# A routed row of 1088 bytes in place of 1032, with the filling written by the operation that writes the row's index

## The chip, the core and the metric

The kernel runs on one core of a Trainium2 chip. The metric is the device time of one execution, in microseconds (us). Engines are named as in the profile: PE (matrix), PEld (its weight loads), DVE (vector), ACT (scalar activation), POOL (GpSimd, which also writes the descriptors of scattering transfers) and SP (which issues most other transfers). Each engine works through its own instructions strictly in their order.

## The reference

```python
def reference(x, filt_r, filt_i, expert_emb, tau, w1, w2):
    # x: (8, 2496, 256); a spectral filter along the sequence
    X = np.fft.rfft(x, axis=1)
    y = np.fft.irfft(X * (filt_r + 1j * filt_i)[None], n=2496, axis=1)
    x = y.reshape(19968, 256)
    # routing to one of 8 experts, each 256 -> 1024 -> 256
    xn, en = x / norm(x), expert_emb / norm(expert_emb)
    logits = xn @ en.T / tau
    expert_idx = argmax(logits, 1)
    gate_w = softmax(logits)[range(N), expert_idx]
    for e in range(8):
        mask = expert_idx == e
        h = maximum(x[mask] @ w1[e], 0)
        out[mask] = gate_w[mask, None] * (h @ w2[e])
    return out
```

## The kernel before

The eight batches are eight groups g = 0 to 7. For each, the spectral filter runs in three stages: `conv_s1` (input transform), `conv_s2` (second transform, the filter and its way back) and `conv_sb` (last transform, then routing). The buffers SD and ZD in DRAM carry data between the stages. `conv_sb` takes a batch in 11 tiles of two blocks of 117 tokens. For a tile, PE makes y; ACT squares the two blocks with a sum (L587, twice, with the operation's result thrown into the part of the row where the low half comes later); DVE makes a power-of-two scale rr from the sums (L590, L592); ACT writes the scaled upper fp16 half into `rows[:, i, 0:D]` (L559, for i = 0 and then i = 1, called first and second scale below); DVE writes the lower half (L562, also twice). POOL's iota (L596) writes the token's index behind the two halves; a reciprocal on DVE (L699) later writes the gate beside it. PE transposes the row (L606) and multiplies it by the experts' embeddings (L621). For every chunk of four tiles, `route` finds the expert and the place, and eight scattering transfers (L711, one for each block, six for the last chunk of three tiles) write the rows into the table XS in DRAM, sorted by expert. They stand as a train on POOL.

The experts' work is done in slots of 256 rows: SP loads a slot's rows from XS with a transposing transfer (xT, L834), PE does the two products (L865 into ph, L892 into po), ACT and DVE make h between them (L871, L872), and POOL scatters the result to the output (L900). While the slots of group g run, the filter of group g+1 runs between them; behind group 7 come slots of 128 rows from what is left over.

At the start no slot can run yet: group 0's filter, `conv_s1` of group 1 and the preparation of the weights (`weight_halves`: maxima on DVE, L242 and L243, an all-reduce over the partitions on POOL, L246, scales and halves on DVE, ACT and POOL, L267 to L272) run alone. This part, some 210 us long, is called the head here. In it the order of ACT and PE is that in which the code is written; everywhere else, and on DVE, POOL and SP throughout, a scheduler orders the instructions. It also derives waits from which bytes of a tile an instruction touches.

A row buffer is `rowp.tile([P, 2, ROW], F16)`: two rows of ROW fp16 numbers behind each other in each partition. Of an XS row, 1024 bytes are the two halves, then 4 bytes of index and 4 bytes of gate.

Of the kernel before, what the change touches and what calls it, by code (L numbers as in the profile page):

```python
# [15 lines left out]
I32 = mybir.dt.int32  # L16
# [9 lines left out]
S = NA * NB39  # L26
NK2 = 20
A3 = 3
TOK = A3 * NB39
NAG = (NA + A3 - 1) // A3  # L30
D = 256
E = 8
F = 1024
ROW = 516

GROUPS = (1,) * 8
QUOTA = 256
# [19 lines left out]
def moe_spectral_kernel(  # L57
# [16 lines left out]
    nc = tc.nc  # L74
# [233 lines left out]
    ZD = [dram.tile([P * NK2, n * D], F32, name=f"ZD{g}") for g, n in enumerate(GROUPS)]  # L308
    XS = dram.tile([XROWS, ROW // 2], I32, name="XS")
    XS16 = XS.bitcast(F16)  # L310
# [13 lines left out]
    def widths(g):  # L324

        return NAG * GROUPS[g] // 2, NK2 * GROUPS[g] // 2
# [20 lines left out]
    def buf_at(g, buf):  # L347
        def at(t, k, half):
            if GROUPS[g] == 2:
                return buf[t * 120:t * 120 + k].rearrange("p (j c) -> p j c", j=2)  # L350
            if half:
                return buf[t * 120:t * 120 + k].unsqueeze(1)
            return buf[t * 240:(t + 1) * 240].rearrange("(j p) c -> p j c", j=2)
        return at
# [4 lines left out]
    def load(q, g, pool, tag, t, ap, rows, full):  # L359
        it = pool.tile([P, 2, D], F32, tag=tag, name=f"{tag}{g}_{t}")  # L360
        got = []
        for h, k, m in whole(g, ap, t, rows, full):
            q.dma_start(it[:k, h], m)  # L363
            got.append((h, it[:k, h].rearrange("p j c -> p (j c)")))
        return got
# [3 lines left out]
    def split(hi, lo, pieces):  # L369

        got = []
        for h, a in pieces:
            k, w = a.shape
            o = h.start * D
            xh, xl = hi[:k, o:o + w], lo[:k, o:o + w]
            nc.scalar.copy(xh, a)
            nc.vector.tensor_tensor(out=xl, in0=a, in1=xh.bitcast(F32), op=ALU.subtract)
            got.append((h, (xh, xl)))
        return got

    def pair(nm):
        return [cw.tile([P, 2 * D], F32R, tag="hl", bufs=XYB, name=f"{nm}_{i}") for i in range(2)]

    def asides(nm):

        return [rowp.tile([P, 2, ROW], F16, tag="rows", name=f"{nm}_{i}").rearrange("p j c -> p (j c)")
                .bitcast(F32R)[:, :2 * D] for i in range(2)]

    def parts_of(c, tag):

        k = c.shape[0]
        tmp = cw.tile([P, P], F32R, tag="hl", bufs=XYB, name=f"{tag}t")[:k]
        lo = const.tile([k, P], F32R, tag=f"{tag}l", name=f"{tag}l")
        nc.scalar.copy(tmp, c)
        nc.vector.tensor_tensor(out=lo, in0=c, in1=tmp.bitcast(F32), op=ALU.subtract)
        hi = const.tile([k, P], F32R, tag=tag, name=f"{tag}h")
        nc.scalar.copy(hi, tmp.bitcast(F32))
        return hi, lo
# [120 lines left out]
    def conv_sb(g):  # L519

        nb = GROUPS[g]
        NTL, _ = widths(g)

        def load_v(t):
            return load(nc.sync, g, cf, "f", t, buf_at(g, ZD[g]), freqs, 120)

        yield W_GAP
        vin = {t: load_v(t) for t in range(3)}
        yield W_GAP
        parts, out_rows = [], []  # L530
        chunks = {}
        yp = {}
        yts = {}

        def part():

            if parts and next(parts[0], None) is None:
                parts.pop(0)
            if out_rows:
                out_rows.pop(0)()  # L540

        if g == G_SB:
            cons["csb"] = parts_of(cons["csb"], "csb")
        for s in range(NTL + LPL):
            if s + 3 < NTL:
                vin[s + 3] = load_v(s + 3)
            if g >= G_SB:
                for u in (0, 1) if s == 0 else (s + 1,):
                    if u < NTL:
                        vin[u] = split(*pair(f"vp{g}_{u}"), vin[u])  # L550
            part()

            t = s - 1
            if 0 <= t < NTL:
                ck = chunks[t // CHUNK]
                rows, rr, y = ck["rows"][t % CHUNK], ck["rr"], yp.pop(t)
                for i in range(2):
                    u = t % CHUNK * 2 + i
                    nc.scalar.activation(rows[:, i, 0:D], y[:, i], AF.Copy, scale=rr[:, u:u + 1])  # L559
                for i in range(2):  # L560
                    u = t % CHUNK * 2 + i
                    nc.vector.scalar_tensor_tensor(out=rows[:, i, D:2 * D], in0=y[:, i], scalar=rr[:, u:u + 1],  # L562
                                                   in1=rows[:, i, 0:D], op0=ALU.mult, op1=ALU.subtract)
            t = s
            if t < NTL:
                c = t // CHUNK
                if t % CHUNK == 0:
                    n = 2 * min(CHUNK, NTL - t)
                    chunks[c] = {
                        "t0": t,  # L570
                        "n": n,
                        "rows": [],
                        "ssq": rt.tile([P, NTC], F32, tag="ssq", name=f"ssq{g}_{t}"),
                        "rr": rt.tile([P, NTC], F32, tag="rr", name=f"rr{g}_{t}"),
                    }
                ck = chunks[c]
                rows = rowp.tile([P, 2, ROW], F16, tag="rows", name=f"rows{g}_{t}")
                ck["rows"].append(rows)
                ssq, rr = ck["ssq"], ck["rr"]
                u = t % CHUNK * 2  # L580
                y = ps_y.tile([P, 2, D], F32, tag="y", name=f"y{g}_{t}")
                for h, vt in vin.pop(t):
                    product(y[:, h].rearrange("p j c -> p (j c)"), cons["csb"], vt)
                yp[t] = y
                for i in range(2):

                    nc.scalar.activation(rows[:, i, D:2 * D], y[:, i], AF.Square, accum_out=ssq[:, u + i:u + i + 1])  # L587

                q = rt.tile([P, 2], I32, tag="q", name=f"q{g}_{t}")
                nc.vector.tensor_scalar(out=q, in0=ssq[:, u:u + 2].bitcast(I32), scalar1=24, scalar2=None,  # L590
                                        op0=ALU.logical_shift_right)
                nc.vector.tensor_scalar(out=rr[:, u:u + 2].bitcast(I32), in0=q, scalar1=-(2.0 ** 23),  # L592
                                        scalar2=194.0 * 2.0 ** 23, op0=ALU.mult, op1=ALU.add)

                (b, ag), _ = tiles(g, t)
                nc.gpsimd.iota(rows.bitcast(I32)[:, :, D:D + 1].rearrange("p j o -> p (j o)"),  # L596
                               pattern=[[S if nb == 2 else TOK, 2]], base=b * S + ag * TOK, channel_multiplier=1)
            yield W_SB
            part()
            t = s - 2  # L600
            if 0 <= t < NTL:
                rows = chunks[t // CHUNK]["rows"][t % CHUNK]
                tp = ps_c.tile([P, 2, 4, P], F16, tag="c", name=f"tp{g}_{t}")
                for i in range(2):
                    for j in range(4):
                        nc.tensor.transpose(tp[:, i, j], rows[:, i, j * P:(j + 1) * P], ident)  # L606
                yT = cy.tile([P, 2, 4, P], F16, tag="yT", name=f"yT{g}_{t}")
                nc.vector.tensor_copy(yT, tp)
                yts[t] = yT

            t = s - LPL
            if t >= 0:
                ck = chunks[t // CHUNK]
                n = ck["n"]
                if t % CHUNK == 0:
                    ck["lp"] = ps_r.tile([P, NTC, 2 * E], F32, tag="r", name=f"lp{g}_{t}")
                for i in range(2):
                    u = t % CHUNK * 2 + i
                    yT = yts[t][:, i]
                    for j in range(4):  # L620
                        nc.tensor.matmul(ck["lp"][:, u], yT[:, j], ent[:, j] if j < 2 else enz[:, j - 2],  # L621
                                         start=(u == 0 and j == 0), stop=(u == n - 1 and j == 3))
                if t % CHUNK * 2 + 2 == n:
                    parts.append(route(g, out_rows, **ck))
            yield W_SB
        while parts or out_rows:
            part()
            yield W_SB
        if g == NG - 1:
            yield from zero_rows(state["base"])  # L630
# [160 lines left out]
    def zero_rows(cnt):  # L791

        zr = cst.tile([P, ROW], F16, tag="st", name="zr")
        nc.vector.memset(zr, 0.0)
# [310 lines left out]
```

## Time and profile before

| what | value |
|---|---|
| median of 3 runs | 1499.54 us (1493.44 to 1501.6) |
| the profiled execution, its own time | 1499.08 us |
| its span, first to last instruction | 1497.2 us |
| PE busy | 1301.8 us, 87% of the span |
| mean granted PE clock | 0.924 of full speed |
| instructions | 31982 |

The profile is one execution. A share of busy time is a mean over the head, the stages with slots and filter side by side, and the end with slots alone.

### The profile page before, as it was taken

To read this page: it belongs to the slowest core of one execution; us is meant where nothing else is said; L and a number is where in the kernel's file an instruction comes from. 1 tells how busy PE (TensorE), PEld (TensorE's weight loads), DVE (VectorE), ACT (ScalarE), POOL (GpSimd) and SP (SyncE) were. 2 spreads that over 40 slices of the span, in tenths; PEclk is the share of its full clock that TensorE was granted. 3 is DMA by queue.
4 is the path that set the end of the run, shared out by engine and by line. 5 is a ranking of instruction groups with operands and counts; after the bars stand their busy time and mean duration, and the time that the engine had idled before them with its cause. 6 is when DMAs were issued, how large, how long until landed. Compare 5 with 4: busy or idle time off the path is not lost.

```text
span 1497.2 us, 31982 instructions
## 1 busy us (share of the span) xinstructions
PE 1301.8 (87%) x10956; PEld 988.2 (66%) x10956; DVE 873.5 (58%) x2841; ACT 693.7 (46%) x1578; POOL 548.7 (37%) x614
## 2 busy tenths in 40 slices
PE   5644557998997998899979988997999789999997
PEld 1212235766765776686658666865787578899997
DVE  2558765563474757575648555664658432266664
ACT  2435554543562665375437634662665122333332
POOL 0021454245524543552445254525433431222222
PEclk7876678999998999999989999999999889999999
DMA  8865375646774775577457746674753222122211
GB/s 273 302 213 200 118 211 158 187 133 189 215 188 130 205 217 156 166 220 183 140 166 201 195 121 185 195 192 124 200 169 92 76 67 54 50 49 48 49 45 40
DMA packets 230494, 229.16 MB, mean 153 GB/s; under 512 B 126089, under 2 KB 172497, under 8 KB 228405
## 3 DMA queue, kind: packets, MB, share of 16 engines
q1 hardware_dynamic: 200908, 151.93, 37.7%
q0 software_dynamic: 26400, 60.07, 12.8%
q10 hardware_dynamic: 3017, 15.02, 3.0%
q8 instruction: 92, 1.51, 0.4%
q14 instruction: 77, 0.63, 0.1%
HBM read 121.61 MB, written 84.84 MB: 138 GB/s over the span
## 4 chain that ended last, share of the span: by engine, by line
PE 61%; issue 15%; POOL 3%; DMA 2%; ACT 1%; DVE 1%; another core or an unknown queue 1%; POOLq 0%; SPq 0%; ACTq 0%; DVEq 0%
PE po L892 22%; PE ph L865 21%; PE y L403 5%; PE s L403 5%; POOL out_dram L900 3%; PE tp L606 2%; PE sa L408 2%; PE s L408 2%; DMA f<-ZD 1%; PE lp L621 1%; PE sa L512 1%; DMA ZD<-z 1%; DVE xs L460 0%; DMA f<-in_filt 0%
## 5 line engine op out<-in xcount | busy, mean ns | idle before, releaser
L892 PE MATMUL po<-W,h 128*128 128x256 f16 (+1 forms) x3864 | 519.8, 279 | 27.9 <-issue 27.5
L892 PEld LDWEIGHTS <-h 128*128 128x128 f16 x3864 | 375.5, 100 | 132.4 <-issue 85.3
L865 PE MATMUL ph<-xT,W 128*128 128x256 f16 x3072 | 414.8, 279 | 30.9 <-issue 18.7
L872 DVE SCALAR_TENSOR_TENSOR h<-ph,h 128x512 f16<-128x512 f32 (+1 forms) x388 | 232.0, 598 | 277.6 <-ACT h L871 240.6
L865 PEld LDWEIGHTS <-W 128*128 128x128 f16 x3072 | 300.1, 100 | 129.0 <-issue 91.4
L871 ACT ACTIVATE h<-ph 128x512 f16<-128x512 f32 (+1 forms) x388 | 203.4, 525 | 378.8 <-PE ph L865 205.4
L900 POOL DMA_INDIRECT out_dram<-o,meta x161 | 171.5, 1065 | 359.0 <-ACT o L899 319.4
L711 POOL DMA_INDIRECT XS<-rows,ixi x176 | 176.6, 1004 | 172.4 <-issue 136.2
L403 PE MATMUL y<-f,csb_sb 120*128 120x512 f32 (+1 forms) x192 | 101.2, 612 | 39.8 <-DVE rows L562 17.7
L494 POOL TENSOR_TENSOR yy<-yy,xs 128x512 f32<-128x512 f32 x70 | 94.3, 1349 | 109.1 <-DVE xs L460 69.5
L363 POOL DMA_DIRECT2D in<-in_x x84 | 66.9, 797 | 154.9 <-PE s L403 113.4
L403 PE MATMUL s<-in,c_sb 117*128 117x512 f32 (+1 forms) x192 | 111.1, 672 | 12.8 <-DMA in<-in_x 8.1
L865 PE MATMUL ph<-xT,wp 128*128 128x128 f16 x1584 | 104.9, 219 | 0.2
L865 PEld LDWEIGHTS <-wp 128*128 128x128 f16 x1584 | 96.7, 98 | 3.2 <-issue 0.7
L587 ACT ACTIVATE rows<-y 128x256 f16<-128x256 f32 x176 | 66.0, 384 | 64.7 <-PE y L403 58.8
L559 ACT ACTIVATE rows<-y,rr 128x256 f16<-128x256 f32 x176 | 73.9, 473 | 46.8 <-DVE rr L592 44.7
L426 ACT COPY s<-s 128x512 f32<-128x512 f32 x88 | 51.5, 586 | 91.4 <-PE s L403 43.5
L458 DVE TENSOR_TENSOR yy<-s,f 128x256 f32<-128x256 f32 x160 | 60.9, 419 | 52.5 <-ACT xs L487 39.4
L562 DVE SCALAR_TENSOR_TENSOR rows<-y,rr,rows 128x256 f16<-128x256 f32 x176 | 77.1, 478 | 22.5 <-ACT rows L559 19.8
L853 DVE COPY wp<-W 128x1024 f16 x132 | 62.1, 471 | 45.3 <-PE ph L865 44.8
L899 ACT ACTIVATE o<-po,meta 128x256 f32<-128x256 f32 x161 | 69.4, 475 | 34.2 <-PE po L892 26.7
L460 DVE SCALAR_TENSOR_TENSOR xs<-xs,sgn_sb,f 128x256 f32<-128x256 f32 x160 | 82.0, 551 | 0.0
(170 smaller groups left out, 1397.0 us busy)
## 6 DMA issues: line engine op xcount, KB each, us to landing
f<-in_filt SPq DMA_DIRECT2D x160, 256.0 KB
a<-SD SPq DMA_DIRECT2D x80, 256.0 KB
ZD<-z SPq DMA_DIRECT2D x80, 256.0 KB
SD<-s SPq DMA_DIRECT2D x80, 240.0 KB
f<-ZD SPq DMA_DIRECT2D x80, 240.0 KB
in<-in_x POOLq DMA_DIRECT2D x70, 234.0 KB
W<-in_w ACTq DMA_DIRECT2D x14, 1024.0 KB
XS<-rows,ixi POOLq DMA_INDIRECT x176
```

Of the source, the lines that this page charges most:

```text
L403: nc.tensor.matmul(out_, c[:a.shape[0]], a, start=True, stop=True)
L460: nc.vector.scalar_tensor_tensor(out=o, in0=i, scalar=sgn_sb[:, k2:k2 + 1], in1=f, op0=ALU.mult, op1=ALU.mult)
L494: nc.gpsimd.tensor_tensor(out=yy, in0=yy, in1=xs, op=ALU.add)
L559: nc.scalar.activation(rows[:, i, 0:D], y[:, i], AF.Copy, scale=rr[:, u:u + 1])
L562: nc.vector.scalar_tensor_tensor(out=rows[:, i, D:2 * D], in0=y[:, i], scalar=rr[:, u:u + 1], in1=rows[:, i, 0:D], op0=ALU.mult, op1=ALU.s ...
L711: i = nc.gpsimd.indirect_dma_start(out=XS, out_offset=bass.IndirectOffsetOnAxis(ap=ix, axis=0), in_=src, in_offset=None)
L865: last["pe"] = nc.tensor.matmul(ph[:, fi, :size], wp[:, k * 2 + wh, fi * P:(fi + 1) * P], xT[:, xh * 2 + k], start=(c == 0), stop=(c == 5))
L871: nc.scalar.activation(h[:, 0, :, :size], ph[:, :, :size], AF.Relu)
L872: hd = nc.vector.scalar_tensor_tensor(out=h[:, 1, :, :size], in0=ph[:, :, :size], scalar=0.0, in1=h[:, 0, :, :size], op0=ALU.max, op1=ALU. ...
L892: nc.tensor.matmul(self.po[:, s], self.hs[fp][:, hh, fi, s * P:(s + 1) * P], self.Wp[:, off + wh * 1024:off + wh * 1024 + D], start=(fp == ...
L899: nc.scalar.activation(o, self.po[:, s], AF.Copy, scale=self.meta[:, s, 1:2])
L900: i = nc.gpsimd.indirect_dma_start(out=out, out_offset=bass.IndirectOffsetOnAxis(ap=self.meta[:, s, 0:1].bitcast(I32), axis=0), in_=o, in_ ...
```

## The change

A row in XS and in the row buffers has 544 fp16 numbers, 1088 bytes, instead of 516 (1032 bytes). The index, which the iota wrote into one 4-byte word of each of the two rows, is now written into all 16 words behind the halves; the gate's reciprocal still overwrites the second of these words later.

```diff
-ROW = 516
+ROW = 544
...
-                nc.gpsimd.iota(rows.bitcast(I32)[:, :, D:D + 1].rearrange("p j o -> p (j o)"),
-                               pattern=[[S if nb == 2 else TOK, 2]], base=b * S + ag * TOK, channel_multiplier=1)
+                nc.gpsimd.iota(rows.bitcast(I32)[:, :, D:],
+                               pattern=[[S if nb == 2 else TOK, 2], [0, ROW // 2 - D]], base=b * S + ag * TOK, channel_multiplier=1)
```

The order of the built instructions, with the engines and queues that each waits for, differs in three places that matter below. In a name such as rows_3_677 the first number is the tile of the batch (here tile 3 of group 0) and the last one only tells buffers apart; the word behind "waits" is the semaphore's owner (Activation is ACT, Pool is POOL, DMAHW and DMASW are transfers).

First, POOL in the head, around the second all-reduce (L246 ISA with wall is the all-reduce; a row that reads ISA alone changes POOL's configuration). Before:

```order
L596 IOTA rows_2_648 128x2
L269 TENSOR_TENSOR W<-W 128x1024 [waits Activation_49]
L596 IOTA rows_3_677 128x2
L246 ISA
L246 ISA wall<-wmax 128x2 [waits DVE_49]
L596 ISA
L596 IOTA rows_4_728 128x2
```

And with the change:

```order
L269 TENSOR_TENSOR W<-W 128x1024 [waits Activation_49]
L596 IOTA rows_1_621 128x2x16 [waits Activation_49]
L596 IOTA rows_2_648 128x2x16 [waits Activation_49]
L246 ISA
L246 ISA wall<-wmax 128x2 [waits DVE_49]
L596 ISA
L596 IOTA rows_3_677 128x2x16 [waits Activation_49]
```

The iota waited for nothing and ran a tile ahead; now each waits for ACT, and that of tile 3 has moved behind the all-reduce and the second change of configuration. The same holds for tile 6 at the third and tile 9 at the fourth such place.

Second, POOL at the first train of group 0, before the change:

```order
L596 IOTA rows_10_1078 128x2
L711 DMA XS<-rows_0_584,ixi_0_967 178304x258 [waits DVE_49] x2
L711 DMA XS<-rows_1_621,ixi_0_967 178304x258 [waits DVE_49]
L711 DMA XS<-rows_1_621,ixi_0_967 178304x258 [waits DMASW7_49,DVE_49]
L711 DMA XS<-rows_2_648,ixi_0_967 178304x258 [waits DMASW0_49,DVE_49]
```

With the change, the end of that train:

```order
L711 DMA XS<-rows_3_677,ixi_0_967 178304x272 [waits DMASW1_49,DVE_49]
L711 DMA XS<-rows_3_677,ixi_0_967 178304x272 [waits DMASW2_49,DVE_49]
L596 IOTA rows_10_1078 128x2x16 [waits Activation_49]
L269 TENSOR_TENSOR W<-W 128x1024 [waits DMAHW1_49,Activation_49,Pool_49]
L711 DMA XS<-rows_4_728,ixi_4_1210 178304x272 [waits DMASW4_49,DVE_49]
```

and ACT at the same tile, with the change:

```order
L587 ACTIVATE rows_10_1078,ssq_8_983<-y_10_1079 128x256 [waits PE_49]
L587 ACTIVATE rows_10_1078,ssq_8_983<-y_10_1079 128x256
L559 ACTIVATE rows_10_1078<-y_10_1079,rr_8_984 128x256 [waits DVE_49]
L559 ACTIVATE rows_10_1078<-y_10_1079,rr_8_984 128x256 [waits Pool_49]
L426 COPY s_8_1147<-s_1_8_1145 128x512 [waits DMAHW2_49,PE_49]
```

The iota of tile 10 has moved from ahead of the train to behind it, and ACT's second scale, which waited for no other engine before, now waits for POOL; in all 88 tiles the second scale has this wait, and in the head its place in ACT's order is the old one. In groups 1 to 7 the scheduler has set the second scale of the last one or two tiles some instructions later in ACT's order (in group 3, tile 10, from ahead of the copies s_7 and s_8 to right behind s_8).

Third, SP where the first slot's rows are loaded (f_8 and f_9 are halves of the filter for `conv_s2`, freed by DVE; names as above):

```order
 L447 DMA f_8_1543<-in_filt 128x512
+L447 DMA f_9_1545<-in_filt 128x512
 L834 DMA_TRANSPOSE xT_0_1397<-XS 128x4x256
 L836 DMA meta_0_1399<-XS 128x2x2
 L834 DMA_TRANSPOSE xT_1_1442<-XS 128x4x256
 L836 DMA meta_1_1444<-XS 128x2x2
-L447 DMA f_9_1545<-in_filt 128x512
```

The filter's load f_9 has moved ahead of xT_0 and xT_1.

## Rows read from the trace of the kernel before

**Rows 1.** The page: the chain that ended last, its share by engine.
```profile
PE 61%; issue 15%; POOL 3%; DMA 2%; ACT 1%; DVE 1%; another core or an unknown queue 1%; POOLq 0%; SPq 0%; ACTq 0%; DVEq 0%
```
**Rows 2.** Windows: stretch, length, busy PE PEld DVE ACT POOL (x), clock, DMA share, GB/s.
```profile
170.00:213.00 43.00, 17.75 (x76) 8.16 (x75) 32.72 (x107) 24.44 (x32) 34.37 (x30) 0.59 0.61 180
213.00:260.00 47.00, 36.72 (x223) 24.71 (x223) 25.51 (x53) 20.45 (x33) 15.82 (x15) 0.89 0.57 167
```
**Rows 3.** Timeline of POOL, head: start, us, instruction [idle before it <-what ended that].
```profile
128.99 0.13 POOL L596 IOTA rows<- 128x2 int32 x1 [7.49 <-issue]
...
141.41 0.37 POOL L246 PARTITION_ALL_REDUCE wall<-wmax  x1 [7.49 <-issue]
149.31 0.22 POOL L596 IOTA rows<- 128x2 int32 x2 [7.53 <-DMA SD<-s]
...
155.42 1.15 POOL L363 DMA_DIRECT2D in<-in_x  x2 [2.26 <-PE s L403]
163.35 0.37 POOL L246 PARTITION_ALL_REDUCE wall<-wmax  x1 [6.78 <-issue]
170.51 0.13 POOL L596 IOTA rows<- 128x2 int32 x1 [6.79 <-issue]
```
**Rows 4.** Timeline of ACT, head: squares L587 and scales L559, tiles 3 to 10.
```profile
125.50 0.47 ACT L559 ACTIVATE rows<-y,rr 128x256 f16<-128x256 f32 x1
...
131.37 0.40 ACT L587 ACTIVATE rows<-y 128x256 f16<-128x256 f32 x1
...
144.53 0.84 ACT L559 ACTIVATE rows<-y,rr 128x256 f16<-128x256 f32 x2 [2.67 <-DVE rr L592]
...
153.55 0.38 ACT L587 ACTIVATE rows<-y 128x256 f16<-128x256 f32 x1
...
166.22 0.84 ACT L559 ACTIVATE rows<-y,rr 128x256 f16<-128x256 f32 x2 [4.97 <-DVE rr L592]
...
170.32 0.84 ACT L559 ACTIVATE rows<-y,rr 128x256 f16<-128x256 f32 x2 [2.31 <-DVE rr L592]
```
**Rows 5.** Timeline of POOL: first train's ends, second train's first, third train's last.
```profile
170.88 1.21 POOL L711 DMA_INDIRECT XS<-rows,ixi  x1 [0.24 <-issue]
...
181.00 0.99 POOL L711 DMA_INDIRECT XS<-rows,ixi  x1 [0.30 <-issue]
...
184.42 1.02 POOL L711 DMA_INDIRECT XS<-rows,ixi  x1 [0.19 <-DVE l L657]
...
204.65 0.90 POOL L711 DMA_INDIRECT XS<-rows,ixi  x1 [0.30 <-issue]
```
**Rows 6.** Timeline of DVE: the places of chunk two, tiles 4 to 7.
```profile
179.55 0.34 DVE L704 CAST ixi<-ix 128x1 int32<-128x1 f32 x4
```
**Rows 7.** Timeline of SP's issues: first slot's rows, then f_9.
```profile
209.65 1.35 SPq L834 DMA_TRANSPOSE xT<-XS  x1
...
213.63 0.40 SPq L447 DMA_DIRECT2D f<-in_filt  x1
```
**Rows 8.** DMA queue of POOL, 1152 to 1168 (one train), 1310 to 1480 (outputs alone).
```profile
q0 software_dynamic: 512, 0.97, 20.1%
q0 software_dynamic: 1536, 3.65, 6.6%
```
**Rows 9.** Groups by line: iota of 2 words in 128 partitions; of 147 in one.
```profile
L596 POOL IOTA rows<- 128x2 int32 x88 | 10.9, 154 | 30.5 <-issue 22.6 <-DMA SD<-s 7.5
L144 POOL IOTA snoi<- 1x147 int32 x1 | 0.3, 253 | 0.0
```
**Rows 10.** Timeline of POOL, group 3: last scatter of its first train.
```profile
594.26 0.98 POOL L711 DMA_INDIRECT XS<-rows,ixi  x1 [0.30 <-issue]
```
**Rows 11.** Timeline of ACT, group 3: scales of tile 10; copy s_8.
```profile
587.42 0.84 ACT L559 ACTIVATE rows<-y,rr 128x256 f16<-128x256 f32 x2
...
599.47 0.58 ACT L426 COPY s<-s 128x512 f32<-128x512 f32 x1 [1.67 <-PE s L403]
```
**Rows 12.** Waits of SP's queue: total us, times, longest.
```profile
SPq L834 <- DMA XS<-rows,ixi: 9.2, 2, 6.1
```

## The prediction

> **What bounds the kernel now.** I read the chain that ended last first. Its shares [rows 1] put 61% of the span on PE, 15% on "issue" (an engine that waits for nothing visible), 3% on POOL, 2% on DMA and 1% each on ACT and DVE. So over most of the span work on ACT, POOL and the queues costs nothing, as long as PE's operands are there. The windows show the exception [rows 2]. From 170 to 213 us PE is busy for 17.75 of 43 us while POOL has 34.37 and DVE 32.72: the end of the head, in which the first rows are scattered and no slot can start. From 213 to 260 us, with the first slots, PE has 36.72 of 47. The rest of the argument is therefore a timeline of POOL, ACT and SP through the head, and a check whether anything like it happens later. The sum is made against the profiled execution, 1499.08 us (a span of 1497.2 and 1.9 around it), 0.5 below the median of 1499.54, so the two need no conversion. About 7.5 us, 0.5%, is what a measurement of this kernel can tell from no change; its three runs lie 8 us apart.
>
> **The bytes.** Rows grow by 56 bytes, 5.4%. A train of scatters with little beside it moved 0.97 MB at 20.1% of 16 engines over 16 us, 51.5 engine-us or 53.0 per MB; the output's rows of 1024 bytes, which are already a multiple of 64, took 6.6% of 16 times 170 us for 3.65 MB, 49.2 per MB [rows 8]. The new train carries 1.02 MB. At 53.0 per MB it costs 54.2, at 49.2 it costs 50.3: between 0.17 us more and 0.08 us less of all 16 engines. Over 22 trains that is -2 to +4 us of queue time, beside other work, since POOL starts one scatter about every 1.4 us whatever the row's length (eight of them from 170.88 to 181.99 [rows 5]). The transposing reads take the same 1024 bytes a row. SP's queue stood behind the scatters twice only, 9.2 us in all, at most 6.1 at once [rows 12]; that is all that sooner landing could give. I take zero.
>
> The Trainium skill ("DMA: Bandwidth & Descriptors", section "How a descriptor splits into AXI transactions") counts a transfer in pieces up to the next boundary of 256 bytes, with whatever lies ahead of an unaligned start also fetched. As an estimate by that page, a row of 1032 bytes averages 36.5 beats and one of 1088 bytes 37: a multiple of 64 alone buys nothing, which speaks against the change's round number. No trace of this kernel alone shows it.
>
> **The iota's own length.** Two words in each of 128 partitions take 154 ns; 147 words in one partition take 253 ns [rows 9]. 32 words in 128 partitions lie between 154 and 253, nearer the second in what each partition writes, less in number; I take 0.2. On POOL that is at most 0.1 us for each of 88 tiles and hidden by its idle time outside the head.
>
> **The new waits.** This is where the change costs. The old iota waited for no square or scale of its tile. With the change it waits for ACT's second square (L587), and ACT's second scale (L559) waits for it. The two touch different bytes; the wait comes from the three-dimensional range of the iota, which as a box also spans the first row's end up to the second row's end. A chain square, iota, second scale now runs through POOL, which works in order. Where POOL is free this fits: ACT has to wait for DVE's rr between square and scale anyway. Where POOL is in something long, ACT stands, and behind it, in order, the copies s for the filter, h's halves and the routing's exponentials.
>
> In the head POOL's idle times ahead of an all-reduce and ahead of the iota behind it are 6.8 to 7.5 us under "issue" [rows 3]: changes of its configuration. The three iotas of tiles 3, 6 and 9 fall behind them:
> - Tile 3: POOL reaches the iota at 128.99 [rows 3] and ends it at about 129.2. The second scale starts then in place of 125.50 [rows 4]: +3.7.
> - Tile 6: tile 5's square ends at 131.77 [rows 4], with +3.7 at 135.5; its iota 0.2, the change 7.49, the all-reduce 0.37, the change 7.53 [rows 3], iota 0.2: 151.3. The pair of scales starts at 144.53, so its second at 144.9 [rows 4]: +6.4.
> - Tile 9: tile 8's square ends at 153.93 [rows 4], about +6: 159.9. Then two loads (1.15), change 6.78, all-reduce 0.37, change 6.79 [rows 3], and the iota of 0.2: 175.2. The second scale of tile 9 was due at 166.22 + 0.42 = 166.6 [rows 4]: +8.6. POOL's first train, behind it, starts 4.6 us later, since the iota that stood ahead of it ended at 170.51 + 0.13 [rows 3].
> - Tile 10: its iota is now behind the train. The train's last scatter ends at 181.99 [rows 5], with +4.6 at 186.6; iota to 186.8. The second scale was due at 170.32 + 0.42 = 170.7 [rows 4]: +16.1. These delays aren't added up: each replaces the former, since ACT idled between.
>
> Next late is DVE's work behind tile 10's lower half and ACT's copies, and with them the places of chunk two, cast at 179.55 [rows 6], if carried in full at 195.6. The second train started at 184.42 [rows 5], 4.9 us after the cast, where POOL had a weight product and waits in between; of 16.1 us 16.1 - 4.9 = 11.2 remain, 11.4 with 0.2 for longer iotas. From there to 205.55 POOL was back to back [rows 5], so the third train and the landing of the first slot's rows go by the same. SP's transfer of xT_0 was issued at 209.65 [rows 7]: +11.4 if that landing decides. But f_9 now stands ahead of it on SP, and f_9 was issued at 213.63 [rows 7]: if its buffer comes free at the same delay, xT_0 goes at 225.0, +15.4. Middle +13.4. PE's idle 10.3 of 47 us [rows 2] in the next stretch can take back one or two; waits in other batches give one back. **Sum: 13.4 - 1.5 + 1 = +12.9; 1499.1 + 13 = 1512.**
>
> On those changes of configuration the Trainium skill ("GPSIMD Engine Reference", section "2.1 Instruction dispatch") says the first call of freshly loaded code pays a load of about 6 us; the rows' 6.8 to 7.5 us agree in kind and are longer. By the page's figure, an estimate, each would be some 1.5 us shorter and the sum some 3 us less, 1509.
>
> **The other batches.** In groups 1 to 7 the last tile's iota also stands behind a train. In group 3 the train's last scatter ends at 594.26 + 0.98 = 595.24 while the scales were at 587.42 to 588.26 [rows 10, 11]. At the old place in ACT's order the second scale would stand 595.4 - 587.84 = 7.6 us. But there it now follows the copy s_8, which ended at 600.05 [rows 11], 4.8 us after the train. Worked out in the same way for the seven groups the cover is 2.5, 5.1, 4.8, 3.0, 2.5, 7.0 and 2.7 us. So no wait is left unless trains end later than that; with the cover gone it is 5.5 to 8.5 us each, 50.6 together. What is late then is DVE's lower half, the transposes and the last chunk's routing, in slots where PE has other work. I take +1 for all.
>
> **Rivals.**
> 1. *The delay is absorbed.* The second train might be held by POOL or DVE, not by tile 10, or PE's idle time between 213 and 260 us may swallow more than I gave. For it: PE idles 10.3 us there, and 25.25 us before [rows 2]. Against it: that idle time is itself waiting for operands that come later too, and POOL has 8.6 us left of the 43. With the second train late by 16.1 minus twice the slack, 6.3, less 3 taken back: 1502; 1499 to 1506.
> 2. *ACT stands in every batch too.* If trains under slots run 3 to 5 us longer than in the profile, the cover of 2.5 to 5 us is gone and some of the 50.6 appear. PE, which needs ACT for the copies s and the halves of h, then stands for a good part: 13 + 17 to 13 + 50, so 1530 to 1560. Against it: the bytes add 0.17 us a train at most, far from 2.5.
> 3. *Faster.* The rows land sooner for being multiples of 64, which gives back the 9.2 us at SP [rows 12], and the second scale's waits fall into time in which ACT idled (its idle behind PE and DVE in the head is 18.6 of 43 us [rows 2]). That gives 1490. It decides if a train's landing gets shorter by over 3 us and the head moves by less than that. Against it: 53.0 to 49.2 per MB is 0.08 us a train, and the chain through tile 10 is a matter of order, not of bandwidth.
>
> **How the numbers follow.** The head's delay carried through, with its ends +7.5 (more given back) and +21 (16.1 with no slack, f_9's 4 and the 1): 0.62, its own range 1507 to 1520. Absorbed: 0.20. Every batch: 0.10. Faster: 0.08, of which 0.06 lies beyond 0.5%. The range from 1500 to 1526 takes the first case whole and most of the second, and a start of stalls in the batches; it leaves out the other side and the full stall. Within 0.5%: the absorbed case and the 0.02, 0.22. Slower: 0.62 + 0.10 = 0.72.
>
> **What would show it.** In the head, ACT's L559 idle with POOL's L596 as what ended it, about 16 us at tile 10 (over 10: right; under 5: wrong); the iota of tile 10 behind a train; the second train at about 196 in place of 184.4; xT_0 at 221 to 225. From there on everything shifted by one amount, with L559's wait for POOL under 1 us a tile in groups 1 to 7; if those waits are 5 us and more, rival 2. An iota of 0.15 to 0.25 us. If POOL's queue takes much less time for a train, or L834 no longer waits, the bytes matter more than I say. The prediction is wrong if the head ends where it did, or if the shift at 260 us isn't the difference of the totals.

## The result

The change takes 1515.61 us (median of four, 1508.23 to 1518.31) against 1499.88 (four, 1493.44 to 1501.6): a ratio of 1.0104, 95% interval 1.0072 to 1.0137, or 15.7 us slower. The profiled execution took 1508.23 us with a span of 1506.4, the quickest of the four; against the one of before it is 9.1 us longer. So the rows below show where 9 us went, and the other 6.6 lie in executions without a trace.

The chain that ended last, by engine, after the change (compare [rows 1]):

```profile
PE 63%; issue 18%; DMA 7%; DVE 4%; POOL 3%; ACT 2%; another core or an unknown queue 1%; POOLq 0%; SPq 0%; ACTq 0%; DVEq 0%
```

The two stretches at the end of the head and behind it, in the columns of [rows 2]:

```profile
170.00:213.00 43.00, 16.66 (x89) 8.35 (x88) 28.81 (x106) 21.90 (x32) 24.86 (x22) 0.54 0.38 117
213.00:260.00 47.00, 33.20 (x188) 21.80 (x189) 29.72 (x59) 21.90 (x35) 20.58 (x17) 0.81 0.65 197
```

POOL does 9.5 us less work in the first stretch, of which 4.8 turn up in the second: the trains come later. PE's loss is mainly in the second, 33.20 in place of 36.72, and its granted clock there is 0.81 instead of 0.89 (means over the stretch).

POOL's timeline after the change, the rows that answer to [rows 3, 5]:

```profile
118.30 0.37 POOL L246 PARTITION_ALL_REDUCE wall<-wmax  x1 [7.03 <-issue]
125.59 0.16 POOL L596 IOTA rows<- 128x32 int32 x1 [6.91 <-issue]
...
140.35 0.37 POOL L246 PARTITION_ALL_REDUCE wall<-wmax  x1 [7.19 <-issue]
147.42 0.16 POOL L596 IOTA rows<- 128x32 int32 x1 [6.70 <-issue]
...
167.45 0.37 POOL L246 PARTITION_ALL_REDUCE wall<-wmax  x1 [6.63 <-issue]
174.62 0.16 POOL L596 IOTA rows<- 128x32 int32 x1 [6.80 <-issue]
175.03 1.21 POOL L711 DMA_INDIRECT XS<-rows,ixi  x1 [0.25 <-issue]
...
185.28 0.17 POOL L596 IOTA rows<- 128x32 int32 x1
...
196.05 1.00 POOL L711 DMA_INDIRECT XS<-rows,ixi  x1 [5.24 <-DVE l L651]
...
218.54 0.90 POOL L711 DMA_INDIRECT XS<-rows,ixi  x1 [0.30 <-issue]
```

The iotas of tiles 3, 6, 9 and 10 are those at 125.59, 147.42, 174.62 and 185.28. ACT's second scales that waited for them (compare [rows 4]):

```profile
125.78 0.47 ACT L559 ACTIVATE rows<-y,rr 128x256 f16<-128x256 f32 x1 [4.17 <-POOL rows L596]
...
147.62 0.47 ACT L559 ACTIVATE rows<-y,rr 128x256 f16<-128x256 f32 x1 [3.99 <-POOL rows L596]
...
174.81 0.47 ACT L559 ACTIVATE rows<-y,rr 128x256 f16<-128x256 f32 x1 [4.02 <-POOL rows L596]
...
185.49 0.47 ACT L559 ACTIVATE rows<-y,rr 128x256 f16<-128x256 f32 x1 [8.24 <-issue]
```

Each starts 0.2 us after its iota's start, the last too, whose idle time the view puts down to "issue". They stand 20.4 us together. DVE's places of chunk two [rows 6] and SP's load of the first slot's rows [rows 7]:

```profile
195.59 0.34 DVE L704 CAST ixi<-ix 128x1 int32<-128x1 f32 x4
```

```profile
217.01 1.07 SPq L447 DMA_DIRECT2D f<-in_filt  x2
224.17 1.35 SPq L834 DMA_TRANSPOSE xT<-XS  x1
```

So from step to step the lateness against before is: first train 4.2 us (175.03 for 170.88), cast 16.0, second train 11.6, end of the third train 13.9 (219.44 for 205.55), xT_0 14.5. One caution goes with these steps: ACT's first squares began at 101.1 us here and at 103.9 before, and in the fourteen traces of this case they begin anywhere from 100.5 to 107.7, so a single step in the head is known to some 3 us. The first output scatter, in the trace of before and then in this one, is 11.3 us late:

```profile
242.86 1.15 POOL L900 DMA_INDIRECT out_dram<-o,meta  x1 [2.02 <-ACT o L899]
```

```profile
254.19 2.12 POOL L900 DMA_INDIRECT out_dram<-o,meta  x1 [1.55 <-DVE isc L257]
```

Those from 280 to 480 us are some 12.2 late, the last 9.1. The groups of the scale and the iota (answering to [rows 9]):

```profile
L559 ACT ACTIVATE rows<-y,rr 128x256 f16<-128x256 f32 x176 | 75.6, 472 | 69.2 <-DVE rr L592 42.8 <-POOL rows L596 14.2 <-issue 10.8
L596 POOL IOTA rows<- 128x32 int32 x88 | 14.1, 161 | 165.5 <-ACT rows L587 143.9 <-issue 20.8 <-DVE mv L672 0.7
```

16 words for each row in a partition cost 161 ns in place of 154 for one: nothing. Of the scale's waits for POOL only three small ones, 0.9, 2.0 and 1.0 us, lie behind the head; each ends 0.2 us after an iota's start, though the view puts the first and the last down to "issue".

### The profile page after: what moved, and what is told of

Its sections match the earlier page's. It is cut to its first block, busy times and chain, and to the rows that moved or that the text cites. A ratio compares the mean times of both kernels' runs of the same rounds, so it can differ in the third digit from the quotient of the medians.

```text
span 1506.4 us, 31974 instructions
## 1 busy us (share of the span) xinstructions
PE 1302.1 (86%) x10956; PEld 989.6 (66%) x10956; DVE 872.1 (58%) x2841; ACT 694.6 (46%) x1578; POOL 550.5 (37%) x614
## 3 DMA queue, kind: packets, MB, share of 16 engines
q0 software_dynamic: 26400, 61.24, 12.9%
## 4 chain that ended last, share of the span: by engine, by line
PE 63%; issue 18%; DMA 7%; DVE 4%; POOL 3%; ACT 2%; another core or an unknown queue 1%; POOLq 0%; SPq 0%; ACTq 0%; DVEq 0%
PE ph L865 21%; PE po L892 21%; PE s L403 6%; PE y L403 5%; POOL out_dram L900 3%; PE tp L606 3%; PE sa L408 2%; PE s L408 2%; DMA W<-in_w 2%; DMA f<-ZD 2%; PE sa L512 1%; PE lp L621 1%; DMA SD<-s 1%; DVE wmx L242 1%; DMA ZD<-z 1%
## 5 line engine op out<-in xcount | busy, mean ns | idle before, releaser
L865 PE MATMUL ph<-xT,W 128*128 128x256 f16 x3072 | 417.6, 281 | 21.1 <-issue 15.4
L559 ACT ACTIVATE rows<-y,rr 128x256 f16<-128x256 f32 x176 | 75.6, 472 | 69.2 <-DVE rr L592 42.8
L587 ACT ACTIVATE rows<-y 128x256 f16<-128x256 f32 x176 | 65.9, 383 | 69.4 <-PE y L403 64.8
L608 DVE COPY yT<-tp 128x1024 f16<-128x1024 f16 x88 | 60.1, 683 | 34.7 <-remote 16.5
```

Source lines behind the costliest of these rows:

```text
L865: last["pe"] = nc.tensor.matmul(ph[:, fi, :size], wp[:, k * 2 + wh, fi * P:(fi + 1) * P], xT[:, xh * 2 + k], start=(c == 0), stop=(c == 5))
```

## The experiments

The twelve ran in three later sets of four, each set on another chip and beside executions of before on that chip. The first set has the four kernels that tell waits from bytes and head from batches; the second the change itself, the two on the waits of the head and the one with early iotas; the third the two other row sizes, the iota ahead of the squares and the last kernel. In all three before takes 1405 to 1407 us (17 to 29 executions a set) and not 1500. Ratios are to before in the same set; a loss in us is that ratio times before. The times that the first expectations give were made from the comparison above, so only differences can be held against them. No trace of before was taken in the later sets. The kernel with two iotas and 1088 bytes (below), whose order on PE, ACT, DVE and SP is that of before, stands in for it. From 260 to 1200 us the trace of before and then that of this kernel have, in the columns of [rows 2]:

```profile
260.00:1200.00 940.00, 870.00 (x7045) 656.31 (x7044) 564.73 (x2026) 482.83 (x1150) 405.70 (x465) 0.96 0.61 169
```

```profile
260.00:1200.00 940.00, 920.67 (x7863) 725.34 (x7861) 591.48 (x2100) 511.46 (x1201) 437.26 (x566) 0.99 0.63 177
```

So PE gets through its work sooner in the later sets, with a higher granted clock and with less idle time (19 of 940 us for 70). Why the later sets differ so from the first comparison is not shown. First the change itself:

> The change itself, beside the next three on the same chip. If this chip grants PE as much clock as in the last four runs (before at about 1406 us): 20 to 27 us slower, the sum of the waits in group 0 alone (16.2) and in groups 1 to 7 alone (7.0). If it runs as in the first comparison (before at about 1500 us): 12 to 19 us slower, with waits of the second scale for POOL in the head alone.

Measured: 1433.51 us, ratio 1.0193 (1.0170 to 1.0216), some 27 us slower: 1.7 times the loss of the first comparison. The first of the two cases held, at its upper end. The scale's group shows more waits for POOL than the 14.2 us of the first comparison:

```profile
L559 ACT ACTIVATE rows<-y,rr 128x256 f16<-128x256 f32 x176 | 75.8, 473 | 87.0 <-DVE rr L592 44.6 <-POOL rows L596 41.4 <-DVE ssq L156 0.3
```

41.4 us of waits for POOL, half of them outside the head. That at tile 10 is 8.24 us again, and here the view puts it down to the iota.

**Waits or bytes.** Two kernels take the change apart. One keeps 1088 bytes and drops the common range:

```diff
-nc.gpsimd.iota(rows.bitcast(I32)[:, :, D:],
-               pattern=[[S if nb == 2 else TOK, 2], [0, ROW // 2 - D]], base=b * S + ag * TOK, channel_multiplier=1)
+for i in range(2):
+    nc.gpsimd.iota(rows.bitcast(I32)[:, i, D:], pattern=[[0, ROW // 2 - D]],
+                   base=b * S + ag * TOK + i * (S if nb == 2 else TOK), channel_multiplier=1)
```

> The row keeps its 1088 bytes, the filling is written by two iotas of 16 words, one for each of the two rows, so that no range spans the other row's halves; the second scale then waits for no iota, and ACT, PE, DVE and SP have the order of before. Theory (the head's waits through POOL): 1497 to 1504 us, second train of group 0 at about 184 us as before, no idle time of the scale for the iota. Rival (the bytes of the longer rows): 1508 to 1518, as the change.

Measured: 1402.85 us, ratio 0.9984 (0.9967 to 1.0000). No scale waits for POOL; the second train starts at 185.3 us. The other keeps the change's iota and goes back to the short row:

```diff
-ROW = 544
+ROW = 516
```

> Rows of 1032 bytes again, but the index is written by the change's three-dimensional iota over both words behind the halves. Theory (waits): 1508 to 1518 us; ACT's scale stands about 20 us in all in the head, 8 of them at tile 10, and the second train starts at about 196 us. Rival (bytes): 1497 to 1504.

Measured: 1433.63 us, ratio 1.0198 (1.0178 to 1.0218), the same as the change, and outside the expectation, which was made from the loss of the first comparison. The whole loss comes with the common range; the bytes have no part in it. What the common range brings is new waits and, from them, another order: in the traces of before and of the change, some 1100 of PE's 10956 instructions stand at another place in the sequence, nearly all of them behind the head. Two more runs price the bytes with the waits gone, on the kernel with two iotas, with 516 (shown) and with 576:

```diff
-ROW = 544
+ROW = 516
```

> Two iotas, one for each row, with rows of 1032 bytes (2 words each): the same orders and waits as the kernel with two iotas and 1088 bytes, so the difference of the two is the price of the bytes and of their alignment alone. Theory (bytes off the path): within 3 us of before. Rival (aligned rows gain, which hid a part of the loss): 3 us or more slower than the kernel with 1088 bytes, 1406 or more against 1402.9.

> Two iotas with rows of 1152 bytes, 12% more than 1032. Theory (bytes off the path): within 3 us of before, POOL's queue up by 8 to 12% in the time its packets take. Rival (bytes cost where a train's landing is waited for): 3 us or more slower than the kernel with 1088 bytes.

Measured: 1404.97 us at 1032 bytes, ratio 0.9986 (0.9958 to 1.0015); 1408.36 at 1152 bytes, 1.0010 (0.9984 to 1.0036). Three sizes, three ratios whose intervals overlap. POOL's queue in the profile of the kernels with 1032, 1088 and 1152 bytes (packets, MB, share of 16 engines):

```profile
q0 software_dynamic: 26400, 60.07, 13.7%
```

```profile
q0 software_dynamic: 26400, 61.24, 13.9%
```

```profile
q0 software_dynamic: 26400, 62.59, 14.0%
```

Of spans of 1410.0, 1399.0 and 1404.0 us that is 193, 194 and 197 us: +0.7% and +1.8% for 1.9% and 4.2% more bytes of the whole queue. The 8 to 12% expected at 1152 bytes was wrong, as it forgot what else goes through the same queue, the output's rows above all. The Trainium skill ("DMA: Bandwidth & Descriptors", section "How a descriptor splits into AXI transactions") splits a transfer at boundaries of 256 bytes; by the estimate made from it in the prediction a multiple of 64 alone buys nothing. The totals agree with that, 0.9984 at 1088 bytes against 0.9986 at 1032, but as the bytes are off the path, they do not test the rule itself.

**Head or batches.** The same edit, two iotas in place of the change's one, was made for groups 1 to 7 alone (shown), and for group 0 alone (`g == 0`):

```diff
+if g > 0:
+    for i in range(2):
+        nc.gpsimd.iota(rows.bitcast(I32)[:, i, D:], pattern=[[0, ROW // 2 - D]],
+                       base=b * S + ag * TOK + i * (S if nb == 2 else TOK), channel_multiplier=1)
+else:
     nc.gpsimd.iota(rows.bitcast(I32)[:, :, D:],
...
```

> The change's iota in group 0 alone, two iotas of 16 words in groups 1 to 7. Theory (the head carries it all): 1507 to 1517 us, the second train at about 196 us, and the shift of the slots' outputs stays between 10 and 14 us to the end. Rival (part of the loss is stalls in groups 1 to 7): at most half of the change's loss, 1503 to 1508, and the rest in the next kernel.

> Two iotas of 16 words in group 0, the change's iota and with it the other order in groups 1 to 7. Theory (the head carries it all): 1497 to 1504 us, second train at 184 us. Rival (stalls in groups 1 to 7): 1505 to 1512, with idle time of the second scale behind trains in groups 1 to 7.

Measured: with the waits in group 0 alone 1422.02 us, 1.0115 (1.0096 to 1.0133), 16.2 us slower, the second train at 200.6 us (185.3 with two iotas); the outputs' scatters are 15 to 17 us late up to 900 us, against that kernel's execution, and 21.5 at the end, beyond the 10 to 14 expected. With the change's iota in groups 1 to 7 alone 1412.84 us, 1.0057 (1.0039 to 1.0074), 8.0 us: here the rival is right too. But this kernel also has the change's other order there (again some 1100 places on PE against the kernel with two iotas), so the 8.0 us price waits and order together. Its scale waits for POOL behind the head:

```profile
L559 ACT ACTIVATE rows<-y,rr 128x256 f16<-128x256 f32 x176 | 75.3, 473 | 69.5 <-DVE rr L592 47.7 <-POOL rows L601 20.8 <-DVE ssq L156 0.3
```

and one of these waits, in group 3, on ACT and on POOL:

```profile
574.36 0.59 ACT L426 COPY s<-s 128x512 f32<-128x512 f32 x1 [1.40 <-PE s L403]
576.79 0.47 ACT L559 ACTIVATE rows<-y,rr 128x256 f16<-128x256 f32 x1 [1.84 <-POOL rows L601]
```

```profile
566.53 1.05 POOL L716 DMA_INDIRECT XS<-rows,ixi  x1 [2.16 <-issue]
...
575.59 0.98 POOL L716 DMA_INDIRECT XS<-rows,ixi  x1 [0.31 <-DVE l L667]
576.57 0.18 POOL L601 IOTA rows<- 128x32 int32 x1
```

The copy s_8 now ends at 574.95, before the train at 576.57; in the first comparison it ended 4.8 us after it [rows 10, 11]. The train takes 10.0 us in both traces; POOL sets its pace. The cover is made of copies that wait for PE, and it shrinks where PE gets there sooner. The clock is only a part of that. In the trace of before PE stood three times at this place without a visible reason:

```profile
592.35 0.20 PE L621 MATMUL lp<-enz,yT 128*128 128x16 f16 x2 [0.73 <-issue]
593.78 0.20 PE L621 MATMUL lp<-ent,yT 128*128 128x16 f16 x2 [1.23 <-issue]
...
595.21 0.80 PE L892 MATMUL po<-W,h 128*128 128x256 f16 x3 [1.18 <-issue]
```

Here it does not, and the granted clock is 1.00 from 568 to 577 us where before had 0.79 from 586 to 600. What those 3.1 us are is not shown. 16.2 and 8.0 make 24.2, at the lower end of the change's interval of 23.9 to 30.4. Against the kernel with two iotas, whose 0.9984 the sum otherwise counts twice, the two are 18.4 and 10.3 us and the change 29.4: the two parts make up the whole.

**Which wait of the head.** Tile 10 freed (shown, against the kernel with the waits in group 0 alone), and tile 10 alone kept (`t != 10`):

```diff
-if g > 0:
+if g == 0 and t == 10 or g > 0:
```

> The change's iota stays for tiles 0 to 9 of group 0; tile 10 and groups 1 to 7 have two iotas, so the waits at tiles 3, 6 and 9 remain and that behind the train is gone. Theory (each delay replaces the former, tile 10 sets the second train): the first train 4.6 us late as with the change, the second train held by POOL alone, 4 to 6 us late; in all 3 to 8 us slower than before. Rival (the waits add up one by one, tile 10 is 8 of 20 us): 8 to 11.

> Only tile 10 of group 0 has the change's iota, all other tiles have two. Theory: first train at its old time, tile 10's second scale behind it at about 182.4 us, 11 to 12 late; the second train 6 to 9 us late, in all 5 to 11 us slower than before. Rival (the early waits at tiles 3, 6 and 9 carry the loss): under 4.

Measured: 1409.87 us, 1.0024 (1.0007 to 1.0041), 3.4 us slower, and 1412.24, 1.0056 (1.0036 to 1.0076), 7.9 us. Both totals fall where "each delay replaces the former" put them, and neither rival holds. The steps fit less well. In the first kernel the first train starts at 182.4 us and the second at 196.1 (171.8 and 185.3 with two iotas), 10.5 and 10.8 late for 4 to 6; its profiled execution, at 1413.7 us, is one of its slower ones, and its squares began 2.2 us later. So no trace shows a second train that is nearly on time without the wait at tile 10; the totals alone speak for it. In the second kernel the second train is 9.4 late for 6 to 9. The two make 11.3 us and not 16.2. Against the kernel with two iotas they are 5.6 and 10.1 for 18.4, which the intervals, some 2.5 us to each side, can still bring together. The wait at tile 10 is also priced together with another order on SP: both kernels that have it load f_9 ahead of xT_0, and the one without it does not. The second kernel also did a thing that wasn't expected. Its POOL and, below it, ACT:

```profile
165.31 0.37 POOL L246 PARTITION_ALL_REDUCE wall<-wmax  x1 [6.71 <-issue]
165.92 1.21 POOL L716 DMA_INDIRECT XS<-rows,ixi  x1 [0.24 <-DVE wall L249]
...
183.74 0.24 POOL L598 IOTA rows<- 128x16 int32 x2 [7.06 <-issue]
183.93 0.15 POOL L601 IOTA rows<- 128x32 int32 x1
...
194.73 1.21 POOL L716 DMA_INDIRECT XS<-rows,ixi  x1 [5.29 <-DVE ixi L709]
```

```profile
184.11 0.47 ACT L559 ACTIVATE rows<-y,rr 128x256 f16<-128x256 f32 x1 [11.31 <-POOL rows L601]
```

With no iota left between the all-reduce and the first train, the train starts 0.2 us behind the all-reduce and the change of configuration, 7.06 us, follows it. A scattering transfer needs no change; an iota does. The wait at tile 10 grows to 11.31 us by it.

**The place of the iota.** Two kernels keep one iota of 32 words and issue it early, for group 0 at the start of its stage (two iotas elsewhere), or in every tile ahead of the squares:

```diff
+if g == 0:
+    for t in range(NTL):
+        rows = rowp.tile([P, 2, ROW], F16, tag="rows", name=f"rows{g}_{t}")
+        (b, ag), _ = tiles(g, t)
+        nc.gpsimd.iota(rows.bitcast(I32)[:, :, D:],
+                       pattern=[[S if nb == 2 else TOK, 2], [0, ROW // 2 - D]],
+                       base=b * S + ag * TOK, channel_multiplier=1)
+        early.append(rows)
...
```

> The change's iota of 32 words is issued for all 11 tiles of group 0 at the start of its stage, into 11 buffers taken at once; groups 1 to 7 have two iotas. Theory (the place of the iota on POOL is what costs, not its form or bytes): no wait of the second scale, within 4 us of before; the first train no longer stands behind the change of configuration after the third all-reduce and starts up to 7 us earlier, but the change then lies ahead of the weight product before the second train, which starts within 2 us of its old time. Rival (the form or the bytes cost): 10 us or more slower.

```diff
+nc.gpsimd.iota(rows.bitcast(I32)[:, :, D:],
+               pattern=[[S if nb == 2 else TOK, 2], [0, ROW // 2 - D]], base=b * S + ag * TOK, channel_multiplier=1)
 for i in range(2):
     nc.scalar.activation(rows[:, i, D:2 * D], y[:, i], AF.Square, accum_out=ssq[:, u + i:u + i + 1])
...
-nc.gpsimd.iota(rows.bitcast(I32)[:, :, D:],
-               pattern=[[S if nb == 2 else TOK, 2], [0, ROW // 2 - D]], base=b * S + ag * TOK, channel_multiplier=1)
```

> One iota of 32 words a tile as in the change, but issued ahead of the tile's squares, so that the squares wait for the iota and the second scale for nothing. Theory (the order square, iota, scale is what costs): 0 to 6 us slower than before, since the iota no longer waits for the square and runs up to a tile ahead, with some squares waiting where POOL stands in a change of configuration or a train. Rival (any wait of ACT for POOL in a tile costs as much): 15 us or more slower.

Measured: 1417.14 us, 1.0081 (1.0058 to 1.0105), 11.4 slower, with no wait of the scale for POOL; and 1422.15, 1.0116 (1.0076 to 1.0155), also with none, and with squares that wait for PE alone. The second of them has another order in all groups, so its total has that in it too; the first has the order of the kernel with two iotas on PE, ACT and DVE. Both theories fell; the rivals' figures were met but not their reasons, as no wait of the scales or squares for POOL is left and an iota takes 145 ns in the first of them. Its POOL:

```profile
127.63 0.37 POOL L246 PARTITION_ALL_REDUCE wall<-wmax  x1 [6.58 <-issue]
...
144.26 2.12 POOL L269 TENSOR_TENSOR W<-W 128x1024 f16<-128x1024 f32 x1 [10.36 <-ACT rows L567]
...
153.34 0.37 POOL L246 PARTITION_ALL_REDUCE wall<-wmax  x1 [6.03 <-issue]
...
168.70 2.51 POOL L269 TENSOR_TENSOR W<-W 128x1024 f16<-128x1024 f32 x1 [8.15 <-ACT W L271]
...
178.44 0.37 POOL L246 PARTITION_ALL_REDUCE wall<-wmax  x1 [6.00 <-issue]
```

The weights' subtraction L269 is now the first instruction behind each all-reduce that needs the configuration back. POOL stands 8 to 10 us in front of it, the weights' chain with it, and the third all-reduce comes at 178.4 us (164.1 with two iotas, 174.1 in the second of these kernels, where POOL stands 9 to 10 us there too). In before the iota between all-reduce and L269 had started the change while POOL had nothing else to do. The iota was cheap and useful where it stood; ahead of that place it costs as much as behind it. That this is the cause is a reading of these rows; the next run tests it, by taking the subtractions off POOL, with the early iotas; up to the first train, POOL then has nothing that needs a change:

```diff
-nc.gpsimd.tensor_tensor(out=lo, in0=raw, in1=hi, op=ALU.subtract)
+v.tensor_tensor(out=lo, in0=raw, in1=hi, op=ALU.subtract)
```

> As the kernel with the early iotas, and the weights' lower halves (L269) are subtracted on DVE in place of POOL, so that POOL has nothing but all-reduces and transfers in the head and needs no change of configuration between them. Theory (in the head the changes of configuration, 7 us each, set when the trains start, and the iota is dear or cheap by where it stands among them): the third all-reduce some 5 to 10 us earlier than its old time of about 164 us, first train at 158 to 166, the first slot's rows loaded 3 to 7 us earlier, in all 2 to 8 us faster than before. Rival (DVE, busy for 33 of 43 us there, takes the place of POOL): no gain or a loss up to 5 us, with the places of chunk two cast later than 180 us.

Measured: 1397.13 us, ratio 0.9928 (0.9904 to 0.9951), some 10 us faster than before and, by the ratios, 37 faster than the change. Its POOL, DVE and SP:

```profile
119.44 0.34 POOL L246 PARTITION_ALL_REDUCE wall<-wmax  x1 [10.90 <-DVE rr L600]
138.68 1.37 POOL L246 PARTITION_ALL_REDUCE wall<-wmax  x1 [8.31 <-DVE f L666]
157.46 0.35 POOL L246 PARTITION_ALL_REDUCE wall<-wmax  x1 [1.68 <-DVE ixi L714]
158.42 1.74 POOL L721 DMA_INDIRECT XS<-rows,ixi  x1 [0.60 <-DVE sg L165]
...
176.59 0.24 POOL L606 IOTA rows<- 128x16 int32 x2 [7.14 <-DVE ixi L714]
177.06 1.21 POOL L721 DMA_INDIRECT XS<-rows,ixi  x1 [0.23 <-POOL rows L606]
```

```profile
168.84 1.23 DVE L269 TENSOR_TENSOR W<-W 128x1024 f16<-128x1024 f32 x1 [0.32 <-ACT W L268]
```

```profile
199.68 1.35 SPq L844 DMA_TRANSPOSE xT<-XS  x1
```

The idle time ahead of these all-reduces now ends with work of DVE and no longer with "issue". One change seems to be left: POOL stands 7.14 us ahead of the iotas of group 1's first tile, between the first and the second train. The third all-reduce and the first train fall where the theory had them; the first rows are loaded at 199.7 us (210.7 with two iotas), 11 us earlier where 3 to 7 were expected, and the gain is at the upper end or beyond. Not all of the head's gain lasts: the first output comes 14.3 us earlier than in the trace with two iotas, and by 350 us only 5 of them are left. The subtraction takes 1.2 us on DVE for 2.1 on POOL, and the rival, DVE in POOL's place, fell. Taking L269 off POOL is part of this gain, so the run prices the two together; the subtraction on DVE without the early iotas was not run.

## Why the prediction was right, and where not

The forecast of 1512 us and the sum of 12.9 stand: 15.7 by medians, 9.1 in the profiled execution, some 12.2 at the outputs from 280 to 480 us. The sum lies between the two totals, and terms that were off to either side helped it there. The range reached 26.9 us above before, and the 27 us of the later sets lie at or beyond that end, so it was also luck that the first comparison came out on the mild side.

- **The new waits carry the cost.** Shown for the common range: without it 0.9984, with it and the old bytes 1.0198. In the head, where the order hardly changes, it is the waits; behind the head the other order that comes with them is not separated from them. In the first comparison the same order cost nothing there: the lateness fell from 12.2 to 9.1 us.
- **Each delay replaces the former, tile 10 sets the second train.** The totals of the two runs with and without tile 10 bear it out, the steps in their traces only in part. The terms were 3.7, 6.4 and 8.6 us for the scales of tiles 3, 6 and 9 (measured 0.3, 2.7 and 8.2), 4.6 for the first train (measured 4.2), 195.6 for the cast of chunk two (195.59), 11.4 for the second train (11.6), and 16.1 for tile 10's second scale (14.8: 185.49 for 170.7). That the cast agrees to 0.01 us is partly luck, as this execution's squares began 2.9 us earlier than before's; that is also why tiles 3 and 6 seem so little late.
- **Lateness isn't waiting.** The sign I named was 16 us of idle time at tile 10, "over 10: right; under 5: wrong". It was 8.24, because the first scale was itself late. I had confused how late an instruction is with how long its engine stands in front of it; only the first enters the sum.
- **Behind the second train.** 11.4 was to stay 11.4 to xT_0 if landing decides, 15.4 if f_9 does; I took the middle, 13.4. The measured 14.5 comes from neither end: f_9 went out 7 us ahead of xT_0, which followed the third train's end by 4.7 us (4.1 before), so landing decided. But trains two and three, with what POOL did between them, took 23.4 us for 21.1. It isn't the bytes: with the old row and the common range they take 23.3, with 1088 bytes and two iotas 22.0. A mis-sized term, right by accident in the middle.
- **What PE takes back** was put at 1.5 us; from xT_0 to the first output it is 3.2. From there to the end another 2.2 us were given back, where I had added 1 for the other batches.
- **The iota's length** was put at 0.2 us and is 0.16.
- **The other batches.** +1 was about right in the first comparison, where three waits make 3.9 us. But my condition for the rival, trains that run 3 to 5 us longer, was the wrong one. The trains stayed as they were and the cover, paced by PE, got shorter: in the later sets these waits, with the order that goes with them, cost 8 us. Had I asked what paces train and cover, I would have seen that the answer depends on how soon PE gets through its work.
- **Bytes and alignment.** Nothing, as said.
- **The changes of configuration.** Those on tile 9's path were put at 6.78 and 6.79 us; they took 6.63 and 6.80. Counted at 6 us each, as in the estimate of 1509, they would take 1.6 us off the sum and not 3.
- **Absorbed and faster** fell in the first comparison and in the later sets.

Open: why before takes 1500 us in the first comparison and 1405 to 1407 later, and why three of the four executions of the change in the first were 5 to 10 us slower than the profiled one. Two of them report a mean granted clock of 0.912 and 0.913 for 0.920, and no trace of them exists. More waits in the batches, as in the later sets, are possible and not shown. Nor is it shown why the late shift in the run with group 0 alone grew from 16 to 21.5 us behind 850 us; part of it belongs to the execution with two iotas that it is held against, since the kernel without tile 10's wait also falls back by 3 us there.

## What to carry to other kernels

A write whose range spans two rows with a gap is taken as one box by the scheduler, and it gets waits on everything in the gap; look at the waits of the changed instruction and of whatever touches the same tile, not at its bytes. An instruction that waits for almost nothing can be holding an expensive change of state in a harmless place: moved earlier or later, it hands that change to a neighbour that is on the path. Where a wait is covered, ask which engine paces the cover and which the wait, since a chip on which the first is quicker can uncover it.

## What the runs showed that was not expected

- A scattering transfer runs on POOL right behind an all-reduce (0.2 us). Ahead of an iota there POOL stands 6.7 to 7.6 us, and ahead of the two-operand subtraction, where that was the first to need the change, 8 to 10 us.
- The same kernel of before takes 1500 us in one comparison and 1405 to 1407 on the chips of three later sets, and the same change costs 1.0% in the one and 1.9% in the later set that had it.
- 32 words by one iota take 161 ns, two words 154.
